# Batch 1's q and k with four tokens a partition, exponentials summed on ScalarE, other transfer times in the ordering list

## The chip, the cores and the metric

One core of one Trainium2 chip runs the kernel. Its time is device microseconds for one execution; the median of the runs shown is the measure. The profile is one execution taken by the hardware profiler, and all rows below are from it.

## The reference

Attention over q, k, v of shape (8, 8, 576, 64) in two forms whose results are added, and then a feed-forward layer over the 4608 tokens:

```python
# pooled: q, k, v averaged over groups of 4 tokens; softmax attention on 144 tokens; repeated 4 times
out_d = sm_attn(q_d, k_d, v_d)
out_up = np.repeat(out_d, factor, axis=2)
# local: full q, k, v, each token sees tokens less than 4 away
scores = np.where(mask, scale * q @ k.T, -1e9)
attn = exp(scores - max) / (sum + 1e-9)
x = (out_up + attn @ v), heads side by side -> (8, 576, 512)
# feed-forward, 512 -> 2048 -> 512, in float32
xn = (x - mu) / np.sqrt(var + 1e-06) * g_ln
out = x + np.maximum(xn @ w_ch1, 0.0) @ w_ch2
```

The weights come as float64 and are turned to float32 on the chip.

## The kernel before

Work is cut into tasks. Each task has an engine, an estimated duration, tasks it depends on, a due time, and rooms that it takes and gives (76 units of 2 KB a partition in SBUF, eight PSUM banks). A planner (`Plan.order`) simulates the engines with those estimates while the program is written, and what it emits is one fixed order of instructions for each engine. On the chip each engine runs its list in that order and waits on semaphores wherever data is not there. A task estimated too short, or a transfer that lands later than estimated, therefore stops whatever stands behind it in that list. Where TensorE would be idle in the plan during the first 150 us, the planner puts in matmuls on the identity matrix (L216, fillers) ahead of the next real matmul.

For each batch there are four head pairs of pooled attention (`pooled`, `pooled_pair`) and five windows of local attention (`local`, windows numbered 0 to 39 over all batches; window `i` belongs to batch `i // 5`). A window goes through: q and k turned (head dimension on partitions), scores into PSUM (L644 or L658), row maximum on VectorE (L669), exponentials on ScalarE, row sums (L692) and reciprocals on VectorE, division (L698), a transpose by TensorE (L703), the product with v (L721), and the addition to the token block `xt` (L735). In windows outside `BIASED` (4 to 8) VectorE subtracts the maximum from the scores (L675) and two exponentials of 128x256 follow (L684). In windows 4 to 8 the negated, scaled maximum (L672) is the bias of eight exponentials of 128x64 (L688). Pooled attention is alike, with its scaled maximum at L887, its exponentials at L895 and its row sums at L915.

Batch 0 (`b < NPB`, NPB = 1) is loaded by `own_half`: 16 loads of q and k in all, 80 groups of four tokens on partitions, two heads, so runs of 1 KB. TensorE turns each load with eight small matmuls (L499); the turned tile serves both forms of attention, and VectorE sums four tokens from PSUM for the pooled form (L509). The other batches are loaded twice. The pooled form loads q, k and v with four tokens a partition (L794), GpSimd adds them (L807, L808) and TensorE turns the sums (L855). The local form loads each window again: windows 5 to 8 (`i < NPE`, NPE = 9) by rows of one token, runs of 256 B, turned by TensorE (L586); later windows by 32x32 blocks, runs of 128 B, turned by VectorE (L604), with the mask added by VectorE (L664). Windows under NPE get the mask by a matmul (L630). Neighbouring windows overlap, so tokens at their borders are loaded twice.

The feed-forward runs in visits over nine chunks of 512 tokens: nine visits with five of the eight pairs of weight tiles, then nine with the other three. In the first nine, `wide` (L1141) makes the hidden layer and `down` (L1212) the output; the second nine use L1131 and L1212. Float32 products are made of three products in a rounded form, so operands and weights are split in a high and a low part (L389, L395, L1036, L1040). The first visit also needs its weights: 20 pieces loaded by SyncE's queue (L346, L351), turned from float64 by ScalarE (L358) and VectorE (L366, L369) and then split. Chunk 0 needs windows 0 to 4, chunk 1 also windows up to 8.

Due times order the work. For batch 1 they are:

```python
def window_at(i):
    if NWIN <= i < NWIN + NEARLY:
        return w_base + i * w_gap - EARLY      # EARLY = 0
    return w_base + i * w_gap if i >= NWIN else norm_at(i) - B0W
```

## Time and profile before

| what | us |
|---|---|
| median of 3 runs (1051.25 to 1062.53) | 1052.99 |
| the profiled execution | 1054.45 |
| its span, first to last instruction | 1052.7 |
| TensorE busy in the span | 1022.0 |
| VectorE busy | 715.3 |
| ScalarE busy | 404.5 |
| GpSimd busy | 367.2 |

The profiled execution lies 1.5 us above the median and 1.75 us above its own span. The mean granted clock of TensorE is 0.982. The kernel has different limits at its start and later, so the table of stages in the rows is to be read before these totals. A busy TensorE includes fillers.

### The profile page before, as it was taken

Reading aid. Unit: us, or ns where it says so; the run is one execution under the profiler, and the core shown is the slowest. Engines: PE = TensorE matmul, PEld = TensorE weight load, DVE = VectorE, ACT = ScalarE, POOL = GpSimd, SP = SyncE. Lnnn points to the kernel's source line nnn. Section 1 sums busy time; section 2 is a strip of 40 time slices with the busy share of each in tenths; the row PEclk is TensorE's granted clock in tenths of the full one; section 3 lists DMA queues with packets and bytes.
Section 4 is the critical chain, followed back from the end, with each engine's and each line's share of the span. In section 5 each row is a group of like instructions: output and inputs, shape, how many; then the busy total and the mean of one; then the engine's idle time right before and its main releaser. Section 6 shows DMA issues by size and latency. Waiting matters only on the chain.

```text
span 1052.7 us, 21752 instructions
## 1 busy us (share of the span) xinstructions
PE 1022.0 (97%) x8140; PEld 858.4 (82%) x8140; DVE 715.3 (68%) x1562; ACT 404.5 (38%) x1084; POOL 367.2 (35%) x418
## 2 busy tenths in 40 slices
PE   8987789999999999999999999999999999999998
PEld 7776677778788787878787878888889999999997
DVE  4998889757677658668577675454778655566643
ACT  4574554334234233324233332134464443333411
POOL 4476567318435608437245110023122111101100
PEclk8998889999999999999999999999999999999999
DMA  8899775528747466575574352132154132332222
GB/s 174 172 232 212 139 159 102 128 46 145 168 80 147 91 109 150 93 132 131 92 127 122 58 125 58 49 120 81 60 187 151 64 106 94 120 121 93 70 76 85
DMA packets 239898, 122.86 MB, mean 117 GB/s; under 512 B 193264, under 2 KB 217840, under 8 KB 238640
## 3 DMA queue, kind: packets, MB, share of 16 engines
q1 hardware_dynamic: 223200, 80.79, 35.5%
q0 software_dynamic: 12240, 40.14, 14.5%
q8 instruction: 65, 1.06, 0.5%
q10 hardware_dynamic: 4352, 0.53, 0.3%
q14 instruction: 41, 0.34, 0.1%
HBM read 93.06 MB, written 28.31 MB: 115 GB/s over the span
## 4 chain that ended last, share of the span: by engine, by line
PE 88%; DVE 5%; DMA 3%; issue 2%; POOL 1%; SPq 1%; ACT 0%; DVEq 0%; POOLq 0%; ACTq 0%
PE acc L1212 37%; PE h L1141 22%; PE h L1131 13%; PE gs L882 2%; PE lv L721 2%; PE gv L929 2%; PE ls L658 2%; PE gt L901 1%; PE lt L703 1%; PE px L982 1%; DVE cva L369 1%; DMA qn<-in_q_dram 1%; PE lq L499 1%; PE h L216 1%; PE lk L499 1%
## 5 line engine op out<-in xcount | busy, mean ns | idle before, releaser
L1212 PE MATMUL acc<-hiw,hl 128*128 128x512 f32 x576 | 233.6, 406 | 0.0
L1212 PE MATMUL acc<-low,hh 128*128 128x512 f32 x576 | 225.5, 392 | 0.0
L1212 PE MATMUL acc<-hiw,hh 128*128 128x512 f32 x576 | 225.3, 391 | 0.0
L1212 PEld LDWEIGHTS acc<-hiw,hh 128*128 128x128 f32 x576 | 108.1, 188 | 23.7
L1212 PEld LDWEIGHTS acc<-hiw,hl 128*128 128x128 f32 x576 | 108.5, 188 | 21.1 <-issue 1.0
L1212 PEld LDWEIGHTS acc<-low,hh 128*128 128x128 f32 x576 | 108.6, 189 | 17.9
L1156 DVE SCALAR_TENSOR_TENSOR hl<-h,hh 128x256 fp32r<-128x256 f32 x180 | 67.6, 416 | 78.8 <-ACT hh L1149 61.6
L1149 ACT ACTIVATE hh<-h 128x256 fp32r<-128x256 f32 x180 | 59.7, 383 | 142.1 <-PE h L1141 130.4
L1141 PE MATMUL h<-hix,hiw 128*128 128x512 f32 x360 | 111.1, 405 | 0.0
L1141 PE MATMUL h<-hix,low 128*128 128x512 f32 x360 | 103.0, 408 | 2.1 <-DVE low L395 2.1
L1141 PE MATMUL h<-lox,hiw 128*128 128x512 f32 x360 | 97.9, 393 | 1.0 <-DVE lox L1040 1.0
L1192 ACT ACTIVATE hh<-e 128x256 fp32r<-128x256 f32 x108 | 39.1, 410 | 126.3 <-DVE e L1184 101.4
L1141 PEld LDWEIGHTS h<-lox,hiw 128*128 128x128 f32 x360 | 67.9, 189 | 16.8 <-DVE lox L1040 1.7
L1141 PEld LDWEIGHTS h<-hix,low 128*128 128x128 f32 x360 | 65.6, 191 | 16.6 <-DVE low L395 2.5
L1141 PEld LDWEIGHTS h<-hix,hiw 128*128 128x128 f32 x360 | 65.6, 191 | 14.1 <-issue 1.2
L1285 POOL DMA_DIRECT2D parts<-x x36 | 20.2, 563 | 157.6 <-DVE x L1280 155.8
L1082 POOL TENSOR_TENSOR xT<-xf_B,xf_B 128x512 f32<-128x512 f32 x9 | 11.6, 1292 | 153.8 <-ACT xf_B L1068 153.8
L1173 DVE TENSOR_TENSOR e<-h,s 128x512 f32<-128x512 f32 x27 | 18.7, 692 | 51.5 <-PE h L1131 31.3
L1177 DVE TENSOR_TENSOR e<-h,e 128x512 f32<-128x512 f32 x27 | 18.7, 692 | 48.0 <-PE h L1131 47.9
L710 ACT COPY at<-lt 128x512 f32<-128x512 f32 x40 | 23.5, 588 | 59.3 <-PE lt L703 44.6
L1198 DVE SCALAR_TENSOR_TENSOR hl<-e,hh 128x256 fp32r<-128x256 f32 x108 | 43.6, 454 | 2.3 <-ACT hh L1192 0.5
L1131 PE MATMUL h<-hiT,his 128*128 128x256 f32 x216 | 43.5, 283 | 0.0
(279 smaller groups left out, 2112.5 us busy)
## 6 DMA issues: line engine op xcount, KB each, us to landing
s<-in_moe_w_ch_dram SPq DMA_DIRECT2D x64, 256.0 KB
blocks<-xt POOLq DMA_DIRECT2D x9, 1024.0 KB, 4.9
parts<-x POOLq DMA_DIRECT2D x36, 256.0 KB, 2.7
xf_B<-blocks SPq DMA_DIRECT2D x36, 256.0 KB
back<-parts SPq DMA_DIRECT2D x36, 256.0 KB
out_dram<-back SPq DMA_DIRECT2D x36, 256.0 KB
qr<-in_q_dram SPq DMA_DIRECT2D x248, 32.0 KB
v<-in_v_dram SPq DMA_DIRECT2D x62, 128.0 KB
```

The lines of the kernel that those rows point to most:

```text
L499: nc.tensor.matmul(x.p[64 * h2 : 64 * h2 + 64, :, r], lhsT=x.raw[:, h2, r], rhs=ident[:ng, :ng], start=True, stop=True,)
L658: nc.tensor.matmul(x.ps[par][64 * h2 : 64 * h2 + 64, pr], lhsT=x.qt[hs, 2 * pr + h2], rhs=x.kt[hs, 2 * pr + h2], start=True, stop=True,)
L710: nc.scalar.copy(x.at.rearrange("p h j -> p (h j)"), x.pt)
L721: nc.tensor.matmul(x.pv[par][64 * h2 : 64 * h2 + 64, pr], lhsT=x.v[js, head], rhs=x.at[js, pr, 64 * qs : 64 * qs + 64], start=True, stop=True,
L882: nc.tensor.matmul(y.ps[:, c], lhsT=bd[:, c], rhs=y.kt, start=True, stop=True)
L1131: nc.tensor.matmul(side(*PLACE[e]), lhsT=wt[:, k], rhs=xx[:, k], start=n == 0, stop=n == 5)
L1141: nc.tensor.matmul(y.ps[fi], lhsT=wt[a][:, kc * P : (kc + 1) * P], rhs=xx[b], start=n == 0, stop=n == 3 * KC - 1)
L1149: nc.scalar.activation(hh[v, p, th][:, 256 * fi : 256 * fi + 256], side(fi, th), AF.Relu)
L1156: nc.vector.scalar_tensor_tensor(out=hl[v, p, th][:, fs], in0=side(fi, th), scalar=0.0, in1=hh[v, p, th][:, fs].bitcast(F32), op0=ALU.max, ...
L1192: nc.scalar.activation(hh[v, p, th][:, 256 * fi : 256 * fi + 256], place(th, fi), AF.Relu)
L1198: eng.scalar_tensor_tensor(out=hl[v, p, th][:, fs], in0=place(th, fi), scalar=0.0, in1=hh[v, p, th][:, fs].bitcast(F32), op0=ALU.max, op1= ...
L1212: nc.tensor.matmul(acc[v, th][j], lhsT=lt[:, ts], rhs=rt, start=p == 0 and fi == 0 and n == 0, stop=p == npr - 1 and fi == 1 and n == 2,)
```

## The change

NPB goes from 1 to 2 and NPE from 9 to 10: batch 1's q and k are loaded by `own_half` like batch 0's, and windows 5 to 9 take their pieces from the turned tiles. Batch 1's sums over four tokens are made by GpSimd from the turned tile in SBUF (`sums_by_pool`). All exponentials have the negated maximum as bias and write their row sum by ScalarE's accumulator; the scale goes into the copies of k (or into the mask's addition for windows 10 to 39). Batch 1's due times move later by up to 35 us. Windows under NPE may have v loaded from GpSimd's queue. The planner's estimates of transfers and of ScalarE's instructions change. Left out of the diff below: the same kinds of edit to the estimates of other loads (blocks, pooled raw loads, the saving of `xt`), the removal of the three lines of L915's reduction (`shares` in `pooled_pair`), and names passed through.

```diff
@@ -36,10 +36,10 @@
         self.rate, self.moved = 270.0, 0.0
-        self.wire, self.lanes = 1.05, 8
+        self.wire, self.lanes = 2.0, 8
         self.landed, self.soft = [], []
-    def add(self, eng, dur, fn, deps=(), due=0.0, take=(), give=(), lag=None, ahead=1e9, alt=None, kb=0, n=1, more=0.1, late=None):
+    def add(self, eng, dur, fn, deps=(), due=0.0, take=(), give=(), lag=None, ahead=1e9, alt=None, kb=0, n=1, more=0.2, late=None):
@@ -68,7 +68,7 @@
                 takers[room].append((t, n))
-        engines = {e: 0.0 for t in self.tasks for e in t.opts}
+        engines = {e: 0.8 if e == "SP" else 0.0 for t in self.tasks for e in t.opts}
         ready = {e: [] for e in engines}
@@ -191,8 +191,8 @@
     NXT, NXP = 2, 2
-    BIASED = range(4, 9)
-    NPE, NPB = 9, 1
+    DIVIDE = 0.5
+    NPE, NPB = 10, 2
     SEP = {}
@@ -287,19 +287,19 @@
     def window_at(i):
-        if NWIN <= i < NWIN + NEARLY:
-            return w_base + i * w_gap - EARLY
+        if NWIN <= i < 2 * NWIN:
+            return w_base + i * w_gap + LATER1 * (2 * NWIN - i) / NWIN
         return w_base + i * w_gap if i >= NWIN else norm_at(i) - B0W
...
             return norm_at(0) - B0G - B0G_GAP * (3 - pr)
-        return g_base + b * ROUND - (NPAIR - 1 - pr) * (ROUND / NPAIR if b > 1 else G1)
+        return g_base + b * ROUND - (NPAIR - 1 - pr) * (ROUND / NPAIR if b > 1 else G1) + (LATER1 if b == 1 else 0.0)
...
     U_SPARE = 4
-    NEARLY, EARLY = 2, 0
+    LATER1 = 35.0
     G1 = 6
@@ -318,7 +318,7 @@
     def act(n, sbuf=False):
-        return (0.155 if sbuf else 0.14) + n / 1430.0
+        return (0.12 if sbuf else 0.07) + n / 1010.0
@@ -372,7 +372,7 @@
         add = plan.add
-        t = add("SP", 1.0, load, (), due, take=(("u", 3),), lag=LAT, kb=512, n=2, ahead=W_AHEAD)
+        t = add("SP", 1.0, load, (), due, take=(("u", 3),), lag=LAT, kb=460, n=2, ahead=W_AHEAD)
         t = add("ACT", 0.87, high_word, (t,), due)
@@ -512,20 +512,38 @@
                 t = unit([P, 512], f"o{nm}t{b}_{pr}_{half}")
-                own_t[nm, pr, half] = t
-                nc.scalar.copy(t[:, : FACTOR * ng], x.p.rearrange("p g r -> p (g r)"))
-
-            t = add("SP", 0.42, load, (), due - 4.0, take=U, lag=LAT, kb=160, ahead=AHEAD)
-            t = add("PE", 0.5, turn, (t,), due, take=A, give=U)
+                own_t[b, nm, pr, half] = t
+                nc.scalar.activation(
+                    t[:, : FACTOR * ng], x.p.rearrange("p g r -> p (g r)"), AF.Copy, scale=SCALE if nm == "k" else 1.0
+                )
+
+            def sums_by_pool(x=x, nm=nm, pr=pr):
+                key = (b, pr // 2, nm)
+                if key not in gsum:
+                    gsum[key] = unit([P, 2, SD], f"gs{nm}{b}_{pr // 2}")
+                n0 = half * GH - g0
+                t = own_t[b, nm, pr, half][:, FACTOR * n0 : FACTOR * (n0 + GH)].rearrange("p (g r) -> p g r", r=FACTOR)
+                two = unit([P, 512], f"two{nm}{b}_{pr}_{half}")[:, : 2 * GH].rearrange("p (g r) -> p g r", r=2)
+                nc.gpsimd.tensor_add(two, t[:, :, :2], t[:, :, 2:])
+                nc.gpsimd.tensor_add(gsum[key][:, pr % 2, half * GH : (half + 1) * GH], two[:, :, 0], two[:, :, 1])
+
+            t = own_loads[b] = add("SP", 0.49, load, (), due - 4.0, take=U, lag=LAT, kb=172, ahead=AHEAD)
+            t = add("PE", 0.55, turn, (t,), due, take=A, give=U)
             done = gsum_done.setdefault((b, pr // 2, nm), [])
-            done.append(add("DVE", dve(288), sums, [t] + done, due + 1.0, take=() if half or pr % 2 else U))
-            own_done.setdefault((b, half), []).append(add("ACT", act(320), turn_out, (t,), due, take=U, give=A))
-
-    def own_piece(nm, pr, w, par, ds):
+            room = () if half or pr % 2 else U
+            if b == 0:
+                done.append(add("DVE", dve(288), sums, [t] + done, due + 1.0, take=room))
+            t = add("ACT", act(320), turn_out, (t,), due, take=U, give=A)
+            own_done.setdefault((b, half), []).append(t)
+            if b > 0:
+                done.append(add("POOL", pool(144) + pool(72), sums_by_pool, [t] + done, due + 1.0,
+                                take=(("u", 2),) if room else U, give=U))
+
+    def own_piece(b, nm, pr, w, par, ds):
         t0 = window_start(w, par)
...
         t0 -= FACTOR * OWN_G[half][0]
-        return own_t[nm, pr, half][ds, t0 : t0 + 64]
+        return own_t[b, nm, pr, half][ds, t0 : t0 + 64]
@@ -558,17 +576,17 @@
-        def load_v():
+        def load_v(eng=nc.sync):
             x.v = unit([P, H, D], f"v{i}")
...
                 if not by_pe:
-                    nc.sync.dma_start(
+                    eng.dma_start(
                         x.v[64 * par : 64 * par + 64], v[b, :, t0 : t0 + 64].rearrange("h s d -> s h d")
...
                 for h2 in range(2):
-                    nc.sync.dma_start(
+                    eng.dma_start(
                         x.v[64 * h2 : 64 * h2 + 64, NPAIR * par : NPAIR * (par + 1)],
@@ -590,11 +608,13 @@
                     t = unit([P, NPAIR, P], f"l{nm}t{i}")
-                    nc.scalar.copy(t.rearrange("p c t -> p (c t)"), x.p[nm])
+                    nc.scalar.activation(
+                        t.rearrange("p c t -> p (c t)"), x.p[nm], AF.Copy, scale=SCALE if nm == "k" else 1.0
+                    )
                     setattr(x, nm + "t", t)
...
                 t = add("SP", 1.33, lambda src=src, nm=nm: load_rows(src, nm), (), due - 12.0, take=U,
-                        lag=LAT, kb=360, n=2, more=1.0, ahead=AHEAD)
+                        lag=LAT, kb=490, n=2, ahead=AHEAD)
                 t = add("PE", 0.43, turn, (t,), due - 8.0, take=A, give=U)
@@ -618,8 +638,9 @@
             turned.append(last_local.ls)
-        vt = add("SP", 2.75 if by_pe else 1.42, load_v, (), due - 8.0, take=U, lag=LAT, kb=360,
-                 n=4 if by_pe else 2, more=1.0, ahead=AHEAD)
+        vt = add("SP", 2.75 if by_pe else 1.42, load_v, (own_loads[b],) if b == 0 else (), due - 8.0, take=U, lag=LAT, kb=360,
+                 n=4 if by_pe else 2, ahead=AHEAD,
+                 alt=[("POOL", 3.1, lambda: load_v(nc.gpsimd), 0.5)] if by_pe else [])
@@ -661,38 +682,30 @@
         def masked(n):
-            nc.vector.tensor_add(x.ps[n], x.ps[n], mask.unsqueeze(1).broadcast_to([P, NPAIR, 64]))
+            nc.vector.scalar_tensor_tensor(
+                out=x.ps[n], in0=x.ps[n], scalar=SCALE, in1=mask.unsqueeze(1).broadcast_to([P, NPAIR, 64]),
+                op0=ALU.mult, op1=ALU.add,
+            )
         def largest():
-            mx = work.tile([P, H], F32, tag="lmx", bufs=4, name=f"lmx{i}")
+            x.mx = work.tile([P, H], F32, tag="lmx", bufs=6, name=f"lmx{i}")
             for n in range(2):
-                nc.vector.reduce_max(mx[:, NPAIR * n : NPAIR * (n + 1)], x.ps[n], axis=AX.X)
-            if not by_dve:
-                x.mx = mx
-                nc.vector.tensor_single_scalar(out=mx, in_=mx, scalar=-SCALE, op=ALU.mult)
-                return
-            for n in range(2):
-                nc.vector.tensor_sub(
-                    x.ps[n], x.ps[n], mx[:, NPAIR * n : NPAIR * (n + 1)].unsqueeze(2).broadcast_to([P, NPAIR, 64])
-                )
+                nc.vector.reduce_max(x.mx[:, NPAIR * n : NPAIR * (n + 1)], x.ps[n], axis=AX.X, negate=True)
...
             x.a = unit([P, H, 64], f"la{i}")
+            x.r = work.tile([P, H], F32, tag="lr", bufs=8, name=f"lr{i}")
             for n in range(2):
-                a = x.a.rearrange("p (c h) j -> p h c j", h=2)[:, n]
-                if by_dve:
-                    nc.scalar.activation(a, x.ps[n], AF.Exp, scale=SCALE)
-                    continue
                 for pr in range(NPAIR):
                     e = NPAIR * n + pr
-                    nc.scalar.activation(a[:, pr], x.ps[n][:, pr], AF.Exp, scale=SCALE, bias=x.mx[:, e : e + 1])
+                    nc.scalar.activation(
+                        x.a.rearrange("p (c h) j -> p h c j", h=2)[:, n, pr], x.ps[n][:, pr], AF.Exp,
+                        bias=x.mx[:, e : e + 1], accum_out=x.r[:, 2 * pr + n : 2 * pr + n + 1],
+                    )
         def shares():
-            r = work.tile([P, H], F32, tag="lr", bufs=8, name=f"lr{i}")
-            nc.vector.reduce_sum(r, x.a, axis=AX.X)
-            nc.vector.tensor_scalar_add(r, r, 1e-9)
-            nc.vector.reciprocal(r, r)
-            x.r = r
+            nc.vector.tensor_scalar_add(x.r, x.r, 1e-9)
+            nc.vector.reciprocal(x.r, x.r)
@@ -746,11 +759,10 @@
             t = add("DVE", dve(256), lambda: masked(1), (t,), due - 5.0)
-        by_dve = i not in BIASED
-        t = add("DVE", (4 if by_dve else 2.4) * dve(256), largest, (t,), due - 5.0)
-        t = add("ACT", 2 * act(256) if by_dve else 1.6, exps, (t,), due - 5.0, take=U, give=(("a", 2),))
-        t = add("DVE", dve(512) + 0.2, shares, (t,), due - 4.0)
-        t = add("DVE", 1.2 * dve(512), divided, (t,), due - 4.0, alt=[("POOL", pool(512), lambda: divided(nc.gpsimd), 0.5)])
+        t = add("DVE", 2 * dve(256), largest, (t,), due - 5.0)
+        t = add("ACT", 2.0, exps, (t,), due - 5.0, take=U, give=(("a", 2),))
+        t = add("DVE", 0.25, shares, (t,), due - 4.0)
+        t = add("DVE", 1.1 * dve(512), divided, (t,), due - 4.0, alt=[("POOL", pool(512), lambda: divided(nc.gpsimd), DIVIDE)])
         t = add("PE", 0.43, turn_a, (t,), due - 3.0, take=A, give=U)
@@ -865,14 +877,15 @@
             y.kt = work.tile([P, SD], F32, tag="ktg", bufs=2, name=f"ktg{i}_{pr}")
-            nc.scalar.copy(y.kt, y.pt[:, 1])
+            nc.scalar.activation(y.kt, y.pt[:, 1], AF.Copy, scale=POOLED_SCALE)
...
                 hs = slice(64 * h2, 64 * h2 + 64)
-                nc.scalar.copy(
+                nc.scalar.activation(
                     bd[hs, :, h2 * GB : (h2 + 1) * GB],
                     gsum[b, hg, "q"][hs, pr].rearrange("p (c g) -> p c g", c=3),
+                    AF.Copy, scale=POOLED_SCALE / (SCALE if b > 0 else 1.0),
                 )
@@ -883,16 +896,18 @@
             y.mx = work.tile([2 * GB, 3], F32, tag="gmx", bufs=4, name=f"gmx{i}_{pr}")
-            nc.vector.reduce_max(y.mx, y.ps, axis=AX.X)
-            nc.vector.tensor_single_scalar(out=y.mx, in_=y.mx, scalar=-POOLED_SCALE, op=ALU.mult)
+            nc.vector.reduce_max(y.mx, y.ps, axis=AX.X, negate=True)
...
                 y.a = work.tile([2 * GB, 3, SD], F32, tag="ag", name=f"ag{i}_{pr}")
+            y.r = work.tile([2 * GB, 3], F32, tag="gr", bufs=4, name=f"gr{i}_{pr}")
             for c in range(3):
-                nc.scalar.activation(y.a[:, c], y.ps[:, c], AF.Exp, scale=POOLED_SCALE, bias=y.mx[:, c : c + 1])
+                nc.scalar.activation(
+                    y.a[:, c], y.ps[:, c], AF.Exp, bias=y.mx[:, c : c + 1], accum_out=y.r[:, c : c + 1]
+                )
@@ -911,13 +926,10 @@
         def shares():
-            r = work.tile([2 * GB, 3], F32, tag="gr", bufs=4, name=f"gr{i}_{pr}")
-            nc.vector.reduce_sum(r, y.a, axis=AX.X)
             nc.vector.tensor_scalar(
-                out=r, in0=r, scalar1=1e-9, scalar2=float(FACTOR), op0=ALU.add, op1=ALU.mult
+                out=y.r, in0=y.r, scalar1=1e-9, scalar2=float(FACTOR), op0=ALU.add, op1=ALU.mult
             )
-            nc.vector.reciprocal(r, r)
-            y.r = r
+            nc.vector.reciprocal(y.r, y.r)
```

## Rows read from the trace of the kernel before

**Rows 1.** Stages: span, busy time of each engine, clock, DMA share, GB/s.
```profile
0.00:20.00 20.00, 17.35 (x272) 15.54 (x274) 7.50 (x18) 8.39 (x20) 5.87 (x19) 0.90 0.90 191
20.00:50.00 30.00, 28.14 (x490) 23.86 (x486) 27.15 (x72) 17.81 (x55) 14.44 (x18) 0.96 0.78 157
50.00:190.00 140.00, 118.31 (x1001) 99.22 (x996) 125.20 (x241) 74.59 (x213) 92.99 (x96) 0.89 0.83 174
190.00:1052.70 862.70, 858.16 (x6394) 719.81 (x6392) 555.49 (x1234) 303.68 (x797) 253.86 (x287) 1.00 0.44 104
```

**Rows 2.** The same view for fillers alone (L216), PE and weight loads.
```profile
0.00:190.00 190.00, 40.16 (x240) 36.66 (x240) 0.90 0.83 173
```

**Rows 3.** TensorE's waits, 0 to 190 us: total, times, longest.
```profile
PE gt L901 <- ACT la L688: 5.7, 1, 5.7
...
PE lq L586 <- DMA qn<-in_q_dram: 2.7, 1, 2.7
```

**Rows 4.** Groups of VectorE, 20 to 50 us: busy, mean ns, idle before.
```profile
L692 DVE TENSOR_REDUCE lr<-la 128x8 f32<-128x512 f32 x5 | 3.3, 668 | 0.0
L675 DVE TENSOR_TENSOR ls<-ls,lmx 128x256 f32<-128x256 f32 x8 | 3.1, 421 | 0.0
...
L915 DVE TENSOR_REDUCE gr<-ag 96x3 f32<-96x432 f32 x4 | 2.4, 589 | 0.0
...
L887 DVE TENSOR_SCALAR gmx<-gmx 96x3 f32<-96x3 f32 x4 | 1.5, 373 | 0.1
```

**Rows 5.** ScalarE's timeline: exponentials of one window in the two forms.
```profile
34.82 0.67 ACT L684 ACTIVATE la<-ls 128x256 f32<-128x256 f32 x2
...
39.28 1.75 ACT L688 ACTIVATE la<-ls,lmx 128x64 f32<-128x64 f32 x8 [1.64 <-DVE lmx L672]
```

**Rows 6.** Groups of VectorE, 50 to 190 us.
```profile
L915 DVE TENSOR_REDUCE gr<-ag 96x3 f32<-96x432 f32 x8 | 4.7, 585 | 0.4 <-ACT ag L895 0.4
...
L887 DVE TENSOR_SCALAR gmx<-gmx 96x3 f32<-96x3 f32 x8 | 4.3, 532 | 0.3
L692 DVE TENSOR_REDUCE lr<-la 128x8 f32<-128x512 f32 x6 | 4.0, 673 | 0.0
...
L675 DVE TENSOR_TENSOR ls<-ls,lmx 128x256 f32<-128x256 f32 x4 | 1.5, 418 | 0.0
...
L604 DVE STREAM_TRANSPOSE lqt<-qr 128x512 f32<-128x512 f32 x2 | 1.4, 701 | 0.0
```

**Rows 7.** DMA, 0 to 190 us: queue (packets, MB, share), issues with sizes.
```profile
q1 hardware_dynamic: 50976, 24.65, 64.6%
...
qn<-in_q_dram SPq DMA_DIRECT2D x8, 128.0 KB
...
qr<-in_q_dram SPq DMA_DIRECT2D x24, 32.0 KB
...
raw2q<-in_q_dram SPq DMA_DIRECT2D x2, 288.0 KB
```

**Rows 8.** Groups of GpSimd, 0 to 190 us.
```profile
L825 POOL TENSOR_TENSOR vd<-rv 72x128 f32<-72x128 f32 x8 | 3.6, 450 | 0.6
...
L807 POOL TENSOR_TENSOR raw2q<-raw2q 72x512 f32<-72x512 f32 x2 | 2.5, 1262 | 0.0
```

**Rows 9.** One line (L369): duration in ns, smallest, median, largest.
```profile
L369 DVE SCALAR_TENSOR_TENSOR cva<-s,cva x64: 410/424/2241, 50.6 to 789.6; 128x256 int32<-128x256 int32 x64
```

**Rows 10.** Issues of v in SyncE's queue, 0 to 60 us: duration as above.
```profile
L571 SPq DMA_DIRECT2D v<-in_v_dram x24: 601/615/1333, 17.0 to 46.2; - x24
```

**Rows 11.** Groups of TensorE, 0 to 190 us.
```profile
L499 PE MATMUL lq<-ident,qo 80*64 80x80 f32 x128 | 7.1, 256 | 1.1 <-issue 1.0
...
L586 PE MATMUL lq<-ident,qn 128*128 128x128 f32 x16 | 2.9, 311 | 2.7 <-DMA qn<-in_q_dram 2.7
...
L855 PE MATMUL gq<-ident,qd 72*128 72x72 f32 x16 | 2.3, 225 | 0.0
```

**Rows 12.** TensorE's timeline: the first products of chunk 1 and their wait.
```profile
184.33 0.49 PE L1141 MATMUL h<-lox,hiw 128*128 128x512 f32 x1 [0.64 <-DVE lox L1040]
```

More of the change, by code (lines that the diff above doesn't have):

```diff
@@ L472, in attention_then_ffn @@
     local_out = {}
-    own_t, own_done = {}, {}
+    own_t, own_done, own_loads = {}, {}, {}
     OWN_G = ((0, 80), (SD - 80, SD))
@@ L611, in local @@
                     ts.append(add("SP", 2.0, lambda src=src, nm=nm, jb=jb: load_blocks(src, nm, jb, nc.sync), ts,
-                                  due - 14.0, take=() if jb else U, lag=LAT, kb=200, n=4, more=0.8, ahead=AHEAD,
+                                  due - 14.0, take=() if jb else U, lag=LAT, kb=324, n=4, ahead=AHEAD,
                                   alt=[("ACT", 3.2, lambda src=src, nm=nm, jb=jb: load_blocks(src, nm, jb, nc.scalar), LATER)] if i >= ALSO else []))
@@ L635, in of @@
                 if own:
-                    return own_piece(nm, pr, w, par, ds)
+                    return own_piece(b, nm, pr, w, par, ds)
                 return getattr(x, nm + "t")[ds, pr, 64 * par : 64 * par + 64]
@@ L827, in pool4_own @@
                             )
-                        t = add("SP", 0.45, load_own, (), due - 4.0, take=U, kb=170, more=1.0, ahead=AHEAD)
+                        t = add("SP", 0.45, load_own, (), due - 4.0, take=U, kb=170, ahead=AHEAD)
                         t = add("POOL", pool(256) + pool(128), pool4_own, [t, lastg.vd[hg]] + ready.get(nm, [])[-1:], due, give=U)
@@ L832, in pooled_half @@
                     continue
-                t = add("POOL" if b > 1 else "SP", 0.78 if b > 1 else 0.45, lambda load=load, b=b: load(eng=nc.gpsimd if b > 1 else nc.sync), (), due - 4.0, take=STG, lag=LAT, kb=340, more=1.2, ahead=AHEAD)
+                t = add("POOL" if b > 1 else "SP", 0.78 if b > 1 else 0.45, lambda load=load, b=b: load(eng=nc.gpsimd if b > 1 else nc.sync), (), due - 4.0, take=STG, lag=LAT, kb=510, ahead=AHEAD)
                 t = add(
@@ L948, in pooled_pair @@
         )
-        t = add("DVE", 0.7, largest, (t,), due - 5.0)
-        t = add("ACT", 0.79, exps, (t, None if own else lastg.t), due - 5.0, take=U if own else (), give=A)
-        t = add("DVE", dve(432) + 0.2, shares, (t,), due - 4.0)
-        ex = add("DVE", 1.2 * dve(432), divided, (t,), due - 4.0, alt=[("POOL", pool(432), lambda: divided(nc.gpsimd), 0.5)])
+        t = add("DVE", 0.6, largest, (t,), due - 5.0)
+        t = add("ACT", 0.95, exps, (t, None if own else lastg.t), due - 5.0, take=U if own else (), give=A)
+        t = add("DVE", 0.25, shares, (t,), due - 4.0)
+        ex = add("DVE", 1.1 * dve(432), divided, (t,), due - 4.0, alt=[("POOL", pool(432), lambda: divided(nc.gpsimd), DIVIDE)])
         outs = []
@@ L1049, in save @@
                 nc.gpsimd.dma_start(blocks[c], xt[c])
-            saved[c] = add("POOL", BEGUN, save, [op_done[v, kc] for kc in range(KC)], due + 4.0, give=XT, lag=LAT, kb=1024)
+            saved[c] = add("POOL", BEGUN, save, [op_done[v, kc] for kc in range(KC)], due + 4.0, give=XT, lag=LAT, kb=810)
             return
```

## Prediction, made before the changed kernel was run

> **What bounds the kernel now.** I read the table of stages first, because the totals mislead: TensorE is busy for 97% of the span. Divided by stage [rows 1], the last 862.7 us have TensorE busy for 858.2 us at the full clock, while VectorE has 555 and ScalarE 304. There only TensorE's work counts, and taking work from any other engine gives nothing. The first 190 us are different. Their granted clock is 0.90, 0.96 and 0.89 by stage, and of the busy time 40.2 us are fillers [rows 2]. With 17.35 + 28.14 + 118.31 = 163.8 us busy, 26.2 us are idle, and 163.8 - 40.2 = 123.6 us do real work, part of it at the lower clock. So some 66 us of the first 190 are filler or idle, and a change can win only out of these (and the clock).
>
> What holds the start back is VectorE and the loads. From 20 to 50 us VectorE is busy for 27.15 of 30 us, and from 50 to 190 us for 125.2 of 140; the DMA engines are at 0.78 and 0.83 there [rows 1]. TensorE's waits name both: the longest is for an exponential at the end of a VectorE chain (5.7 us), another for batch 1's rows (2.7 us) [rows 3]. ScalarE, with 17.81 of 30 and 74.59 of 140, has room. I call 20 to 50 us stage A (batch 0's attention) and 50 to 190 us stage B (first visit, its weights, batch 1, the start of batch 2).
>
> **The change part by part.**
>
> *Stage A, VectorE.* The accumulator takes away the row sums, 3.3 us for five windows and 2.4 us for four pooled pairs. The bias form takes away the subtractions, 3.1 us for windows 0 to 3. The negated maximum takes away the scaling, 1.5 us [rows 4]. Sum 10.3 us of 27.15. Against it ScalarE does eight narrow exponentials for two wide ones, 1.75 us for 0.67 [rows 5], so 1.08 us more in each of windows 0 to 3, 4.3 us: 17.81 becomes 22.1 us. The accumulator's own price is in no row. It lies between nothing and, with the narrowest group that reads and writes as many partitions, 1.75 / 8 = 0.22 us for each instruction; 5 x 8 + 4 x 3 = 52 instructions make 0 to 11.4 us. I take 0.05 us, 2.6 us, because the sum rides on a result already in the engine, so that the lower end is nearer. ScalarE then has 24.7 us of work and VectorE 16.9. ScalarE sits at the head of each chain with 0.82 of the stage's length, so it becomes the next limit: the stage can hardly become shorter than 24.7 us, a gain of 30 - 24.7 = 5.3 us. Bounds: 0 (the accumulator at its upper end: 33.5 us of ScalarE work, which would even lengthen the stage by 3.5 us) to 10.3 us. I take 5.
>
> *Stage B, VectorE.* Six row sums of windows (4.0 us) and eight of pooled pairs (4.7), eight scalings (4.3) and four subtractions (1.5) go away. Of the four block transposes, window 9's two go away: 0.7 us of the 1.4 for q, and as much for k, together 1.4 [rows 6]. Sum 15.9 us of 125.2. The masks of windows from 10 on take one instruction of the same shape as before, so nothing.
>
> *Stage B, loads.* Batch 1 loses eight loads of rows of q and as many of k at 128 KB in runs of 256 B (8192 packets), window 9's 16 block loads at 32 KB in runs of 128 B (4096 packets), and eight pooled loads of q and k at 288 KB in runs of 1 KB (2304 packets) [rows 7]. It gains 16 loads of two heads by 80 groups, 160 KB each in runs of 1 KB (2560 packets). Net 12032 packets and 2304 KB (2.36 MB) fewer. The queue's 50976 packets and 24.65 MB took 64.6% of 16 engines for 190 us, which is 122.7 us of all sixteen [rows 7]. Priced by bytes the relief is 2.36 / 24.65 x 122.7 = 11.7 us, by packets 12032 / 50976 x 122.7 = 29 us. Either is enough that the loads do not fall behind a VectorE that is 15.9 us faster. It is no second gain: the two lie beside each other.
>
> *GpSimd.* It loses eight pairs of additions for batch 1, each 1.26 us [rows 8] and a half-size one of some 0.7 us: 16 us. It gains 16 pairs on 144 and 72 elements. The nearest row, 128 elements in 0.45 us [rows 8], gives 0.5 + 0.3 us, 13 us. So the sums cost nothing net (bounds: -16 to +5 us of GpSimd time, on an engine with 93 of 140 us busy). VectorE is slowed beside GpSimd: L369 has a median of 424 ns and a largest of 2241 [rows 9]. With GpSimd's work about equal I count no change for it.
>
> *v from GpSimd's queue.* Each issue holds SyncE's queue for 0.615 us, and batch 0's 20 come from 17.0 us on [rows 10]. By that row 20 x 0.615 = 12.3 us of issue time could leave SyncE. The DMA engines, though, are at 0.90 in the first 20 us [rows 1], so I count 0, with 2 us as the upper bound (the 10% that is not busy). The Trainium skill, "DMA: Bandwidth & Descriptors", section "Issuing engines are not separate DMA queues", says that DMAs from any engine run on the same 16 DMA engines, and that a second issuing engine saves only issue time. By it the part is worth nothing; by the issue row alone the sum would be up to 12.3 us larger. The busy share agrees with the page.
>
> *TensorE.* Turning a batch by `own_half` took 7.1 us for q and as much for k; four windows by rows took 2.9 and as much; pooled transposes of two batches took 2.3 for q, so 2.3 for q and k of one batch [rows 11]. Net 14.2 - 5.8 - 2.3 = +6.1 us, partly at the low clock. It lies where 66 us are filler or idle, so I cost it at nothing. If that cover is gone it costs 6 us.
>
> *The order.* Batch 1's due times move by 35 us for the pooled part and 35, 28, 21, 14 and 7 us for windows 5 to 9. The first visit's products and weights come ahead of them in every list. The estimates of row loads rise (360 to 490) and the fixed wire time from 1.05 to 2.0 us, so consumers stand further behind their loads. The wait for batch 1's rows (2.7 us) should go. I count nothing beyond that, as it lies inside stage B's sum. The change adds no wait of its own except that GpSimd's sums wait for ScalarE's copy of the turned tile; behind them stand GpSimd's divisions and its issues of later loads.
>
> *Sum.* Stage A gives 5 us. In stage B I let 10 of the 15.9 us through, since VectorE is busy for 0.89 of it and the rest of the time it waits for others; the bounds are 0 and 15.9. After 190 us nothing changes, because TensorE has no idle time and its list holds the same work. 1054.45 - 15 = 1039.5 us for an execution like the profiled one, and 1053.0 - 15 = **1038 us** for the median, which lies 1.5 us lower.
>
> **The rivals.** (1) *All of VectorE's relief arrives*, and with the loads' relief the clock rises too: 10.3 + 15.9 = 26.2 us, 1027 us; with 2 us of v and some of the 0.10 of clock that is missing, 1020. For it: VectorE at 0.9 in both stages. Against: ScalarE takes 24.7 us of stage A. (2) *The gain is hidden.* The accumulator's price is near its upper end, ScalarE becomes the limit of stage A, and stage B is held by the loads of the weights, which the change does not touch: 0 to 5 us, 1050. Against: L688's form is already fast; for it: ScalarE's chain feeds everything. (3) *Slower: chunk 1 comes late.* Window 8 is the last that chunk 1 needs, and it moves 14 us later in every list. Already now the first products of chunk 1 wait for their operands at 184 us [rows 12]. Between the first visit's end and chunk 1's operands TensorE has nothing else to do. If window 8's chain ends 14 us later and little of the relief (2 us) reaches that chain, because the first visit's weights set the pace ahead of it, chunk 1 starts 12 us later: 1053 + 12 = 1065; with 9 us of relief it is 1058. It decides once the delay of window 8 on the chip exceeds the relief ahead of it, some 15 us. Against it: batch 1's work costs fewer engines less time, and the delay is one of due times, not of work.
>
> **How the numbers follow.** Forecast 0.42, rival 1 0.21, rival 2 0.17, rival 3 0.20. The range takes in rival 1's time and rival 3's lower half and leaves out rival 3's upper half and accidents below 1020: 1020 to 1062 us. A measurement of this kernel can tell 1% from no change, so the bounds are 1042.5 and 1063.5 around 1053. Faster by over 1%: all of rival 1 and four fifths of the forecast, 0.21 + 0.34 = 0.55. Slower by over 1%: six tenths of rival 3 and a little of accidents in the order, 0.12 + 0.02 = 0.14. Within 1%: 0.31.
>
> **What would show it.** In the changed profile, rows of L692, L675, L887 and L915 have no successors, and VectorE's busy time up to the same point of work (the last wait for chunk 1's operands) falls by about 26 us, to some 134 of 160. The first product of the hidden layer begins about 5 us earlier, and the stretch from which TensorE is never idle begins at 175 instead of 190 us. The exponentials with accumulator show the price of the accumulator: over 0.27 us each within a train of eight and rival 2 gains. SyncE's queue shows 16 loads of 160 KB more. The forecast is wrong if TensorE's waits in stage B grow (rival 3 names chunk 1's operands), if ScalarE is busy for over 0.95 of stage A, or if after 190 us TensorE is idle or has more busy time than before.

## The result, and the profile after

| | before | changed |
|---|---|---|
| median of 15 runs (range), us | 1060.22 (1051.25 to 1064.52) | 1046.71 (1040.17 to 1050.40) |
| the profiled execution, us | 1054.45 | 1048.63 |
| its span, us | 1052.7 | 1046.8 |
| mean granted clock of TensorE | 0.982 | 0.989 |

The ratio is 0.9885, with a 95% interval from 0.9855 to 0.9915: 12 us of 1060 (9 to 15). The changed kernel run again beside the last experiments gave 0.9922 (0.9893 to 0.9952). Runs of the kernel before scatter over 14 us, so the intervals of single kernels are 0.2 to 0.5% to either side. Nothing smaller is settled by one of them. The two profiled executions differ by 5.8 us, half of what the runs differ by: that of before is one of its faster executions, that of the changed kernel one of its slower.

The stages of the changed kernel's profile answer to [rows 1], with the same columns:

```profile
0.00:20.00 20.00, 17.80 (x319) 16.04 (x319) 9.47 (x22) 11.03 (x31) 4.75 (x17) 1.00 0.89 185
20.00:50.00 30.00, 23.68 (x337) 20.73 (x334) 15.79 (x37) 21.88 (x116) 22.40 (x29) 0.89 0.90 175
50.00:190.00 140.00, 124.36 (x1304) 102.96 (x1305) 105.93 (x221) 86.42 (x308) 94.81 (x122) 0.94 0.63 152
190.00:1046.80 856.80, 849.63 (x6356) 713.24 (x6354) 500.96 (x1097) 357.95 (x1262) 257.54 (x291) 1.00 0.45 105
```

VectorE's work in the first 190 us fell from 159.85 to 9.47 + 15.79 + 105.93 = 131.19 us, and the DMA share of 50 to 190 us from 0.83 to 0.63. Yet TensorE is busy for less of 20 to 50 us than before, 23.68 against 28.14 us. What is gained must therefore lie in the third row. To see how much, I count feed-forward products done by 190 us. The first two lines are the kernel before (L1141, L1212), the next two the changed kernel (L1153, L1224); the first count in a line is that of matmuls:

```profile
0.00:190.00 190.00, 38.14 (x133) 26.12 (x134) 0.90 0.83 173
...
0.00:190.00 190.00, 15.92 (x60) 10.74 (x60) 0.90 0.83 173
```

```profile
0.00:190.00 190.00, 38.53 (x144) 26.71 (x144) 0.94 0.70 159
...
0.00:190.00 190.00, 21.94 (x80) 15.03 (x81) 0.94 0.70 159
```

193 products stand against 224. Four follow four others after 0.91 us where TensorE does nothing else, so 31 are 7.0 us of lead:

```profile
197.31 1.07 PE L1153 MATMUL h<-hix,low 128*128 128x512 f32 x4
198.21 1.07 PE L1153 MATMUL h<-hix,hiw 128*128 128x512 f32 x4
```

The spans differ by 5.9 us. After 190 us TensorE is busy for 849.6 us instead of 858.2, 8.5 us less, and idle for 856.8 - 849.6 = 7.2 us instead of 4.5, 2.6 us more. The products are most of the work that is no longer left at 190 us, and idle time later takes part of the lead back.

Stage A shows why its part is missing. VectorE's groups there (compare [rows 4]) have no row sums and no subtractions left, and VectorE now waits for TensorE. Some of its work has only moved out of the stage: of the additions into `xt` (L748 now; L735 before, in the line by itself) one stands there instead of eight.

```profile
L693 DVE TENSOR_REDUCE lmx<-ls 128x4 f32<-128x256 f32 x10 | 3.8, 417 | 4.2 <-PE ls L665 4.2
...
L748 DVE TENSOR_TENSOR xt<-lv,xp 128x232 f32<-128x232 f32 x1 | 0.4, 399 | 7.8 <-PE lv L734 7.8
```

```profile
L735 DVE TENSOR_TENSOR xt<-lv,xp 128x232 f32<-128x232 f32 x8 | 2.7, 392 | 0.8 <-PE lv L721 0.8
```

TensorE's timeline shows what it waits for itself. Between two transposes of batch 0's windows (L716) stands batch 1's first turning (L499), and its load is not there. A second idle stretch, 4.4 us up to 68.83 us, lies in the same turning; for that one the profile names no releaser ("issue"):

```profile
36.27 0.60 PE L716 MATMUL lt<-ident,la 128*128 128x128 f32 x4
36.71 0.83 PE L216 MATMUL lq<-ident 128*128 128x128 f32 x6
43.34 1.33 PE L499 MATMUL lq<-ident,qo 80*64 80x80 f32 x16 [5.79 <-DMA qo<-in_q_dram]
44.60 1.12 PE L716 MATMUL lt<-ident,la 128*128 128x128 f32 x4
...
47.86 0.60 PE L716 MATMUL lt<-ident,la 128*128 128x128 f32 x4
...
68.83 1.19 PE L499 MATMUL lk<-ident,ko 80*64 80x80 f32 x13 [4.39 <-issue]
```

The load was issued at 32.28 us and its data was used at 43.34. SyncE's queue shows what it stood behind, 16 issues of v and two of weights:

```profile
17.39 12.88 SPq L589 DMA_DIRECT2D v<-in_v_dram  x16
30.32 1.92 SPq L346 DMA_DIRECT2D s<-in_moe_w_ch_dram  x2
32.28 0.46 SPq L490 DMA_DIRECT2D qo<-in_q_dram  x1
```

The clock falls in the idle time. In the ten microseconds from 40 us it is 0.66, a mix of the 1.2 and 2.4 GHz levels, after 1.00 in the ten before. The same lines have the DMA engines' share, the last number but one:

```profile
20.00:30.00 10.00, 9.47 (x148) 7.84 (x146) 7.35 (x18) 8.79 (x40) 9.58 (x15) 1.00 0.53 109
30.00:40.00 10.00, 7.54 (x120) 6.58 (x116) 6.29 (x15) 10.00 (x69) 8.86 (x11) 1.00 1.05 206
40.00:50.00 10.00, 6.67 (x73) 6.31 (x74) 2.15 (x5) 3.09 (x12) 3.96 (x5) 0.66 1.12 210
```

From 20 to 30 us, while the issues of v ran, the DMA engines were busy for 0.53 of the time, so up to its issue the load stood behind the queue and not behind the engines. After its issue it still took some 10.6 us (32.74 to 43.34) until TensorE used it, with the engines at 1.05 and 1.12. How the wait divides between the two is not shown.

The second line also has ScalarE busy for all of 10 us. The price of the accumulator is in its groups of 20 to 50 us. Each exponential is followed by an instruction of its own that reads the accumulator, and the pair overlaps:

```profile
L701 ACT ACTIVATE la<-ls,lmx 128x64 f32<-128x64 f32 x40 | 11.9, 383 | 0.0
L701 ACT ACTIVATION_READ_ACCUMULATOR la<-ls,lmx 128x1 f32 x40 | 10.6, 278 | 0.0
```

An exponential with its readout takes 11.9 / 40 = 0.30 us of the engine's time; without, it took 1.75 / 8 = 0.22 us [rows 5].

### The profile page after: what moved, and what is told of

Read it like the earlier page. It is cut to its first block, busy times and chain, and to the rows that moved or that the text cites. A ratio compares the mean times of both kernels' runs of the same rounds, so it can differ in the third digit from the quotient of the medians.

```text
span 1046.8 us, 22580 instructions
## 1 busy us (share of the span) xinstructions
PE 1015.5 (97%) x8308; PEld 853.0 (81%) x8308; DVE 632.1 (60%) x1375; ACT 477.3 (46%) x1714; POOL 379.5 (36%) x458
## 4 chain that ended last, share of the span: by engine, by line
PE 84%; DMA 6%; DVE 5%; SPq 2%; issue 2%; ACT 1%; DVEq 0%; ACTq 0%
PE acc L1224 36%; PE h L1153 20%; PE h L1143 13%; PE lv L734 2%; DMA qo<-in_q_dram 2%; PE gs L895 2%; PE ls L679 2%; DMA qr<-in_q_dram 2%; PE lt L716 1%; PE px L994 1%; PE gv L941 1%; PE gt L916 1%; DVE cva L369 1%; DMA kr<-in_k_dram 1%; SPq L566 1%
## 5 line engine op out<-in xcount | busy, mean ns | idle before, releaser
L1224 PE MATMUL acc<-hiw,hl 128*128 128x512 f32 x576 | 234.3, 407 | 0.0
L1224 PE MATMUL acc<-low,hh 128*128 128x512 f32 x576 | 226.2, 393 | 0.0
L1224 PE MATMUL acc<-hiw,hh 128*128 128x512 f32 x576 | 225.8, 392 | 0.0
L1224 PEld LDWEIGHTS acc<-hiw,hh 128*128 128x128 f32 x576 | 108.4, 188 | 23.8
L1224 PEld LDWEIGHTS acc<-hiw,hl 128*128 128x128 f32 x576 | 108.9, 189 | 21.7 <-issue 0.8
L1224 PEld LDWEIGHTS acc<-low,hh 128*128 128x128 f32 x576 | 108.9, 189 | 17.8
L701 ACT ACTIVATE la<-ls,lmx 128x64 f32<-128x64 f32 x320 | 95.1, 333 | 45.5 <-DVE lmx L693 34.6
L1153 PE MATMUL h<-hix,hiw 128*128 128x512 f32 x360 | 109.3, 402 | 0.0
L1153 PE MATMUL h<-hix,low 128*128 128x512 f32 x360 | 101.5, 404 | 0.5 <-DVE xt L748 0.3
L1153 PE MATMUL h<-lox,hiw 128*128 128x512 f32 x360 | 97.4, 392 | 0.6 <-DVE lox L1052 0.6
L1153 PEld LDWEIGHTS h<-lox,hiw 128*128 128x128 f32 x360 | 67.6, 188 | 16.2 <-DVE lox L1052 1.3
L1153 PEld LDWEIGHTS h<-hix,low 128*128 128x128 f32 x360 | 65.3, 190 | 14.0 <-issue 0.8
L1153 PEld LDWEIGHTS h<-hix,hiw 128*128 128x128 f32 x360 | 65.1, 189 | 13.6 <-issue 0.8
L701 ACT ACTIVATION_READ_ACCUMULATOR la<-ls,lmx 128x1 f32 x320 | 72.0, 227 | 0.0
```

Source lines behind the costliest of these rows:

```text
L701: nc.scalar.activation(x.a.rearrange("p (c h) j -> p h c j", h=2)[:, n, pr], x.ps[n][:, pr], AF.Exp, bias=x.mx[:, e : e + 1], accum_out=x. ...
L1153: nc.tensor.matmul(y.ps[fi], lhsT=wt[a][:, kc * P : (kc + 1) * P], rhs=xx[b], start=n == 0, stop=n == 3 * KC - 1)
L1224: nc.tensor.matmul(acc[v, th][j], lhsT=lt[:, ts], rhs=rt, start=p == 0 and fi == 0 and n == 0, stop=p == npr - 1 and fi == 1 and n == 2,)
```

## The experiments

Theory A was that work taken from VectorE, and second from the loads, carries the gain, and that the wait above gives some of it back. Theory B was that the loads carry it, theory C that the new order of the lists does. Each kernel was timed beside the kernel before. The first four shared a chip, so did the second four and the last four; the kernel before had medians of 1054.80, 1058.79 and 1054.72 us there.

| run | ratio to before | 95% interval | median, us |
|---|---|---|---|
| softmax edits alone | 0.9895 | 0.9864 to 0.9927 | 1045.08 |
| all but the softmax edits | 0.9926 | 0.9894 to 0.9959 | 1049.30 |
| changed, old estimates | 0.9908 | 0.9875 to 0.9941 | 1046.43 |
| changed, batch 1's turning behind | 0.9855 | 0.9816 to 0.9894 | 1041.51 |
| changed, no accumulator | 0.9892 | 0.9849 to 0.9934 | 1046.17 |
| changed, due times unmoved | 0.9868 | 0.9824 to 0.9912 | 1043.98 |
| old softmax, turning behind | 0.9878 | 0.9831 to 0.9924 | 1045.76 |
| changed, turning further behind | 0.9852 | 0.9809 to 0.9896 | 1042.26 |
| estimates alone | 1.0031 | 1.0008 to 1.0055 | 1058.10 |
| due times alone | 1.0056 | 1.0021 to 1.0091 | 1063.20 |
| changed kernel again | 0.9922 | 0.9893 to 0.9952 | 1046.88 |
| turning behind, again | 0.9886 | 0.9851 to 0.9922 | 1040.47 |

**The softmax edits alone.** The kernel before with the bias form, the accumulator and the scale in the copies:

```diff
-                nc.scalar.activation(a[:, pr], x.ps[n][:, pr], AF.Exp, scale=SCALE, bias=x.mx[:, e : e + 1])
+                nc.scalar.activation(
+                    x.a.rearrange("p (c h) j -> p h c j", h=2)[:, n, pr], x.ps[n][:, pr], AF.Exp,
+                    bias=x.mx[:, e : e + 1], accum_out=x.r[:, 2 * pr + n : 2 * pr + n + 1],
+                )
...
-            nc.vector.reduce_sum(r, x.a, axis=AX.X)
```

> The kernel before with only the softmax edits (bias form, accumulator, scale in the copies, with their own durations in the planner); loads, due times and transfer estimates as before. Theory A (VectorE's relief carries the gain, and batch 1's single load gives some of it back through a wait in stage A): 8 to 15 us faster than before, VectorE's busy time from 0 to 190 us down by 20 us or more. Theory B (the loads carry it): within 4 us of before, though VectorE's busy time falls as much. Theory C (the transfer estimates in the ordering list carry it): within 4 us of before.

It is as fast as the whole change. By 190 us its profile has 168 + 73 = 241 feed-forward products, 48 more than before, which is 10.9 us (L1136 and L1207; its span is 10.1 us shorter than that of before):

```profile
0.00:190.00 190.00, 44.77 (x168) 30.77 (x168) 0.95 0.89 180
...
0.00:190.00 190.00, 21.71 (x73) 14.62 (x74) 0.95 0.89 180
```

VectorE's busy time by 190 us, though, is 9.90 + 17.79 + 123.79 = 151.5 us, 8 us less than before and not 20: with more of the later work reached by then, the comparison at a fixed time was badly chosen. Theory A's time came, its sign of VectorE did not; that the softmax edits alone bring no more than 4 us, as theories B and C had it, is excluded.

**All but the softmax edits.** The changed kernel with the old softmax put back, the rest of the change kept:

```diff
-    DIVIDE = 0.5
+    BIASED = range(4, 9)
     NPE, NPB = 10, 2
...
-                        bias=x.mx[:, e : e + 1], accum_out=x.r[:, 2 * pr + n : 2 * pr + n + 1],
...
+            nc.vector.reduce_sum(r, x.a, axis=AX.X)
```

> The changed kernel with the old softmax (subtraction, VectorE row sums), but batch 1 loaded once, its due times moved and the new estimates. Theory A: within 4 us of before, or slower, with VectorE again at 0.9 in stage A. Theory B or C: 8 us or more faster than before, as the changed kernel is.

0.9926 is 7.8 us of 1054.8, with an interval from 4.3 to 11.2 us. Theory A's "within 4 us" is missed, and the 8 us of theories B and C are within reach. VectorE is busy for 23.76 of 30 us in stage A, 0.79 and not 0.9:

```profile
20.00:50.00 30.00, 27.15 (x388) 22.47 (x384) 23.76 (x64) 16.51 (x53) 16.34 (x25) 0.97 0.94 188
```

The loads' part, with its order, is worth something by itself, and the two parts do not add up: 1.05% and 0.74% alone, 1.15% together.

**The old estimates.**

```diff
-        self.wire, self.lanes = 2.0, 8
+        self.wire, self.lanes = 1.05, 8
...
-        return (0.12 if sbuf else 0.07) + n / 1010.0
+        return (0.155 if sbuf else 0.14) + n / 1430.0
```

> The changed kernel with the old transfer estimates, the old estimate of ScalarE's instructions and v on SyncE's queue alone. Theory A and B: 8 to 13 us faster than before, as the changed kernel. Theory C: no gain or a loss, with more waits of TensorE for DMA in the first 190 us.

The gain stays, so it does not need the new estimates or v on GpSimd's queue. TensorE has no wait for batch 1's qo in this kernel, and its granted clock is 1.00 from 20 to 50 us; yet the first hidden-layer product comes at 74.30 us and the time is no better than the changed kernel's:

```profile
20.00:50.00 30.00, 29.70 (x440) 25.84 (x440) 17.27 (x44) 24.76 (x128) 18.89 (x24) 1.00 1.00 193
```

```profile
74.30 1.75 PE L1152 MATMUL h<-hix,low 128*128 128x512 f32 x4
```

**Batch 1's turning behind batch 0.**

```diff
-            t = own_loads[b] = add("SP", 0.49, load, (), due - 4.0, take=U, lag=LAT, kb=172, ahead=AHEAD)
+            t = own_loads[b] = add("SP", 0.49, load, (), due - 4.0, take=U, lag=LAT, kb=172, ahead=AHEAD, more=0.2 if b == 0 else 6.0)
```

> The changed kernel with 6 us more in the planner's estimate of each of batch 1's own loads, which puts their turning in TensorE's list behind batch 0's transposes and products; nothing else is edited. Theory A: the 5.8 us wait for qo at 37 to 43 us goes, the first hidden-layer product comes 4 to 8 us earlier than at 72.1 us, and the time falls by 3 to 6 us below the changed kernel. Rival D (stage A's end is hidden, since the first visit waits for its weights anyway): the wait goes, the time stays within 2 us of the changed kernel.

The wait for qo is gone. The first hidden-layer product comes at 59.16 us, 13 us before the changed kernel's 72.11, more than the 4 to 8 expected. Part of batch 1's turning (L499) now stands behind it. The granted clock is 1.00, the 2.4 GHz level, from 20 to 190 us:

```profile
47.39 1.96 PE L994 MATMUL px<-ident,xt 128*128 128x128 f32 x16
49.28 0.78 PE L499 MATMUL lq<-ident,qo 80*64 80x80 f32 x16
...
59.16 1.17 PE L1153 MATMUL h<-hix,low 128*128 128x512 f32 x4
...
60.73 0.77 PE L499 MATMUL lk<-ident,ko 80*64 80x80 f32 x16
```

```profile
20.00:50.00 30.00, 27.73 (x482) 24.54 (x481) 21.18 (x51) 23.91 (x119) 24.49 (x30) 1.00 0.95 181
50.00:190.00 140.00, 130.88 (x1330) 106.35 (x1329) 108.50 (x226) 90.28 (x327) 91.16 (x120) 1.00 0.73 164
```

The ratio, 0.9855, overlaps that of the changed kernel. So both were run again on one chip:

> The changed kernel again, to stand on the same chip beside the next one: 10 to 14 us faster than before by the ratio already measured, 0.9885.

> The fourth experiment's kernel again beside the changed kernel. If the wait for batch 1's first load costs the end time what it costs stage A: 3 to 6 us faster than the changed kernel here. If it is mostly hidden behind the first visit's weights: within 2 us of it.

Medians of 1046.88 and 1040.47 us, seven and six runs; their means differ by 4.5 us with a standard error of 2.0. Over all runs of the two kernels (22 and 12, of which fifteen of the changed kernel's were not taken beside the other) the means are 1046.2 and 1041.1 us with standard deviations of 3.4 and 3.9 us, a difference of 5.1 us with a standard error of the square root of 3.4² / 22 + 3.9² / 12, 1.3 us. Putting batch 1's turning behind gains about 5 us, theory A's 3 to 6. How much of that is the wait is not separated. The edit also shortens the second idle stretch (4.4 us before, 1.3 us here), keeps the clock up, and takes part of the turning from in front of the first visit. The kernel with the old estimates speaks against giving all of it to the wait: it has no such wait either, and on the same chip its six runs have a mean of 1046.6 us against this kernel's 1040.8, 5.8 us more with a standard error of 1.8.

**No accumulator.** VectorE sums again, the bias form stays:

```diff
-                        bias=x.mx[:, e : e + 1], accum_out=x.r[:, 2 * pr + n : 2 * pr + n + 1],
+                        bias=x.mx[:, e : e + 1],
...
+            nc.vector.reduce_sum(x.r, x.a, axis=AX.X)
```

> The changed kernel without the accumulator: VectorE sums the exponentials again (with its time in the planner), while the bias form and the scale in the copies stay. If the accumulator carries its share of VectorE's relief (10 of some 26 us by the rows before), a third to a half of the gain goes: 3 to 7 us slower than the changed kernel. If its readout on ScalarE (0.07 us for each exponential) takes as much as it gives: within 2 us of the changed kernel, with ScalarE's stretch of exponentials in stage A shorter by 3 us.

0.9892: the accumulator, put on top of the rest, gives nothing that can be measured, though by the two intervals 3 us are not excluded. Its 40 exponentials of stage A take 8.8 us of ScalarE instead of 11.9, the 3 us expected:

```profile
L701 ACT ACTIVATE la<-ls,lmx 128x64 f32<-128x64 f32 x40 | 8.8, 390 | 0.0
```

This kernel still has a wait for batch 1's load (4.3 us), so the run does not say what the accumulator would give without it.

**Due times unmoved.**

```diff
-    LATER1 = 35.0
+    LATER1 = 0.0
```

> The changed kernel with batch 1's due times where they were (35 us becomes 0), so its turning and its pooled part stand further ahead in every list. Rival 3 (moving them later makes chunk 1 late): faster than the changed kernel by 5 us or more, with fewer waits for chunk 1's operands. The forecast's view (the move keeps batch 1 out of the first visit's way): slower than the changed kernel by 3 to 10 us, with more waits for batch 1's loads before the first hidden-layer product.

Neither came: 0.9868, within the changed kernel's interval, though the first hidden-layer product stands at 90.56 us instead of 72.11:

```profile
90.56 1.20 PE L1153 MATMUL h<-hix,low 128*128 128x512 f32 x4
```

When the first visit starts is not what the end time hangs on: by 190 us this kernel has done 162 + 66 = 228 products, the changed one 224.

**Old softmax, turning behind.** The second experiment's kernel with the fourth's edit:

> The kernel of the second experiment (old softmax, batch 1 loaded once) with the 6 us more in the estimate of batch 1's own loads, as in the fourth. If the two parts add up once the wait is out of the way, this lies 5 to 9 us below before and the fourth experiment's kernel another 6 to 9 us below this one. If they hide each other (VectorE's relief and the loads' relief shorten the same stretch), it lies within 3 us of the fourth experiment's kernel.

0.9878 beside the fourth's 0.9855 and 0.9886: for the most part they hide each other. VectorE's relief gives little more once the loads' part is there without its wait; the next kernel, which has both and ran on the same chip, lies 0.26% lower, within the two intervals.

**Turning further behind**, 12 us instead of 6 in the same line:

> The fourth experiment's kernel with 12 us instead of 6 us more in the estimate of batch 1's own loads. If batch 1's loads are still what TensorE's list meets too early: another 1 to 4 us faster. If the wait was all there was: within 1.5 us of the fourth experiment's kernel, or slower because chunk 1 then waits for batch 1.

0.9852, as the fourth's 0.9855: putting the turning further behind gives nothing more.

**Order alone.** Two kernels with the work of before and only its order changed, by the estimates and by the due times:

```diff
-        self.wire, self.lanes = 1.05, 8
+        self.wire, self.lanes = 2.0, 8
```

> The kernel before with nothing but the new estimates in the planner (transfers, ScalarE, SyncE's start): the same work in another order. Theory A (work taken from VectorE and from the loads carries the gain): within 4 us of before. Theory C (the order alone carries it, and each edit gained because it reordered the lists): 8 us or more faster than before, as the single parts were.

```diff
-        if NWIN <= i < NWIN + NEARLY:
-            return w_base + i * w_gap - EARLY
+        if NWIN <= i < 2 * NWIN:
+            return w_base + i * w_gap + LATER1 * (2 * NWIN - i) / NWIN
```

> The kernel before with nothing but batch 1's due times moved later by up to 35 us: the same work in another order. Theory A: within 4 us of before. Theory C: 8 us or more faster. Rival 3 (chunk 1 comes late): 5 us or more slower, with longer waits for chunk 1's operands near 184 us.

Both are slower, by 0.3% and 0.6%, so theory C's 8 us come from neither of these edits. It is not shut out altogether: every experiment also reorders the lists, because its durations go into the planner, and the fourth gained 5 us by order alone. How much of the 11 us of the softmax edits is work taken away and how much is order, no run here separates.

The first of the two also shows how far a count of products goes: it has 120 + 96 = 216 of them by 190 us, 23 more than before, and yet its span is 7.3 us longer. TensorE still has 860.1 us of work after 190 us, against 858.2 before, and 9.9 us idle against 4.5.

The second is as slow as rival 3 said, 5.9 us (2.2 to 9.6), and not within theory A's 4 us. Its profile, one of the two fastest of its ten executions, does not show rival 3's place: the longest waits in the whole trace are in the pooled attention, and the one for operands of a hidden layer (`lox`, 1.2 us) ends at 62.20 us, not near 184:

```profile
PE gv L929 <- ACT agt L911: 7.9, 2, 7.6
PE gt L901 <- DVE ag L923: 7.8, 5, 3.5
PE gv L929 <- POOL vd L808: 5.6, 1, 5.6
...
PE h L1141 <- DVE lox L1040: 1.2, 1, 1.2
```

In the changed kernel TensorE has no wait for chunk 1's operands up to 200 us. Rival 3's time came for the due times alone; its place is shown in neither kernel.

## Why the prediction held, step by step

**The end.** 15 us (1.4%) were forecast, 9 to 15 us (1.15%) came; the absolute 1038 us was off mostly because the three runs of before that it stood on had a median 7 us below that of fifteen. The size is in part luck: by the two profiles the terms make 7 us and not 15: stage A, which was to give 5 us, lost 3 (the first product of the hidden layer came at 72.11 us instead of 69.06, and not 5 us earlier), and stage B gave its 10. The profiles differ by 5.9 us, the runs by 12; no term explains the rest, and the two profiles lie on the near sides of their spreads.

```profile
69.06 1.20 PE L1141 MATMUL h<-hix,low 128*128 128x512 f32 x4
```

```profile
72.11 2.05 PE L1153 MATMUL h<-hix,low 128*128 128x512 f32 x4
```

One of the signs of being wrong came, too: after 190 us TensorE was to have no idle time, and it has 7.2 us (4.5 already before).

**VectorE's terms** were near. 26.2 us were to go, 28.7 went by 190 us, a comparison at a fixed time, which the first experiment shows to be rough. Stage A was to have 16.9 us and has 15.79, but some 2 us of that are the additions into `xt` that now come later.

**ScalarE's term.** The price of the accumulator, 0.05 us for each, was a choice between 0 and 0.22; the measured 0.08 us is nearer the lower end. ScalarE did become full in a part of stage A, in 30 to 40 us; over the stage it is busy for 21.88 of 30 us.

**The loads.** q1's packets fell from 50976 to 34352 and its share from 64.6% to 50.7% [rows 7]:

```profile
q1 hardware_dynamic: 34352, 21.25, 50.7%
q0 software_dynamic: 2819, 8.60, 18.5%
```

That is 122.7 - 96.3 = 26.4 us of all sixteen engines in the queue, against 29 us foretold by packets and 11.7 us by bytes. But 16624 packets and 3.4 MB went, more than the 12032 and 2.36 MB that were counted. For what went, the price by packets is 16624 / 50976 x 122.7 = 40 us and by bytes 3.40 / 24.65 x 122.7 = 17 us, so the measured relief lies between the two prices. Some of it only moved: 12 of the 40 v loads of windows 0 to 9 went to the other queue.

**The sum of stage B.** "It is no second gain: the two lie beside each other" is what the runs bear out, more strongly than it was meant: either relief alone brings about as much as both. 31 products by 190 us are 7.0 us; from a start 3 us later they are the 10 us that stage B was given.

**The step that failed is stage A's 5 us.** Batch 0's token block reached its first transposes (L994, L982 before) at 54.84 instead of 50.12 us. I had counted "nothing beyond" the order and named only whom GpSimd's new wait would hold. TensorE's list got a new wait too: batch 1's turning in the middle of batch 0's transposes, on a load that stands behind 16 issues of v, 12.88 us together. The same mistake is in the v term. I let the busy share of the DMA engines decide that issue time is worth nothing, and took the 0.90 of the first 20 us, though the issues run from 17.0 to 46.2 us [rows 10], where the share was 0.78. I did so with a page of the Trainium skill that agreed, "DMA: Bandwidth & Descriptors", section "Issuing engines are not separate DMA queues": a second issuing engine saves only issue time. For bandwidth that may be so. For the one load that TensorE waits for, the 12.9 us of issues ahead of it in SyncE's queue come first, and the DMA engines were at 0.53 from 20 to 30 us meanwhile. Only 4 of batch 0's 20 issues of v went to GpSimd's queue. The run with the old estimates, where all 20 stay on SyncE's queue, has no wait of TensorE for qo in its order, and in the fourth experiment the load stands behind the same 16 issues without one, so the place in TensorE's list decides, not the queue alone. What that place costs the end time is the 5 us of the fourth experiment; the wait's own share of it stays open.

**Smaller terms.** GpSimd's sums cost 4.1 + 4.0 + 2.8 + 2.8 = 13.7 us (13 forecast). TensorE's turning of two batches took 13.3 us for q against 7.1 for one, so 6 us more for each of q and k (7.1 forecast). That it was covered is not shown. TensorE is idle or on fillers for 190 - 165.83 + 32.6 = 56.8 us of the first 190 instead of 66, but from 56.74 to 70 us batch 1's turning stands right in front of the first visit, and the fourth experiment, which moved part of it behind, was faster.

```profile
L527 POOL TENSOR_TENSOR twoq<-oqt 128x144 f32<-128x144 f32 x8 | 4.1, 509 | 8.8 <-ACT oqt L516 8.8
...
L528 POOL TENSOR_TENSOR gsq<-twoq 128x72 f32<-128x72 f32 x8 | 2.8, 355 | 0.6
```

**The rivals.** Rival 2's limit, ScalarE full, came for ten of stage A's thirty microseconds and without its result. Rival 3 did not come in the changed kernel. Rival 1 (1027 us) did not come even with the wait removed (about 1041): not all of VectorE's relief arrives. What stage B then waits for is not settled by these runs; in the fourth experiment VectorE still has 108.5 of 140 us, ScalarE 90 and GpSimd 91 there, none of them full.

## What to carry to other kernels

When lists are ordered ahead of time, ask of every moved load which instruction of the busiest engine first needs it and what stands behind that one: here a load that came 6 us late for its place in TensorE's list stood where some 5 us were lost. Two reliefs of the same stretch can be worth about the larger one, as here, so run each alone before paying for both. And compare progress instead of busy time at a fixed time, since a faster kernel has reached other work by then; count all the work that TensorE has left, because one kind of product alone pointed the wrong way once here.

## What the runs showed of the hardware

The accumulator of an exponential is read by an instruction of its own on ScalarE, 0.20 to 0.35 us long (median 0.28 us for 128x64), which overlaps its neighbours so that each 128x64 exponential takes 0.30 instead of 0.22 us. After an idle stretch of 5.8 us TensorE's granted clock was 0.66 in the ten microseconds from 40 us; where the wait was taken away it stayed at 1.00 there. While 16 issues of v, 64 KB each, took 12.88 us of SyncE's queue, the DMA engines were busy for 0.53 of 20 to 30 us. Putting nothing but the order differently moved these kernels by 0.3 to 0.6%.
